# Float64 weights of a two-stage MoE: more raw chunks with places of their own, low parts subtracted by GpSimd, the factor 256 taken out of the split

## The chip, the cores and the metric

The kernel runs on one core of a Trainium2 chip. The metric is the device time of one execution in microseconds (us), smaller is better. The core has five engines with a queue each, run in order: TensorE (PE, with the weight load shown as PEld), VectorE (DVE), ScalarE (ACT), GpSimd (POOL) and SyncE (SP), which here issues the DMAs. Engines wait for each other through semaphores.

## The reference

```
def _moe_ref(x, w_a, w_b, w_out):
    a = x @ w_a
    b = x @ w_b
    return (a * b @ w_out).astype(np.float32)

def _moe2_ref(x, w_gate, w_val, w_out):
    gate = 1.0 / (1.0 + np.exp(-(x @ w_gate)))
    val = x @ w_val
    return (gate * val @ w_out).astype(np.float32)

def reference(**kwargs):
    attn_out = _attn_ref(**attn_kwargs)
    x = attn_out.transpose(0, 2, 1, 3).reshape(B * S, H * D)
    x = _moe_ref(x=x, **moe_kwargs)
    return _moe2_ref(x=x, **moe2_kwargs)
```

An attention of 4 batches, 8 heads, 576 positions of 64 (half of the heads see a local band of 32 positions, the other half every 32nd position) feeds two mixtures of 2304 tokens, 512 features and 1536 hidden features. The weights of both arrive as float64. The change is in the first mixture, a * b @ w_out.

## The kernel before, in words

**Tiles.** Tokens are worked in five tiles (four of 4 x 128 tokens, one of 4 x 64). For each tile the first mixture loops over 12 chunks k of 128 hidden features. Each chunk has three weights m of 128 x 512: m = 0 for a, m = 1 for b, m = 2 for the output. A product in fp32 accuracy is made of three passes in the type fp32r: high weight times high input, low weight times high input, high weight times low input, so each weight and each input is split in a high and a low part. On TensorE a chunk is 12 matmuls for a, 12 for b (line 1133) and 12 for the output (line 1224), the last for the chunk before.

**Conversion.** `convert` (line 495) turns each float64 weight into two fp32r parts, in the first tile only; the parts stay in 12 zones of SBUF, zone k for chunk k, and are used again by the later tiles. One weight goes through: `load` on SP (line 524, a DMA of 512 KB raw), `top` on ScalarE (530, the upper bits as a float), `merge` on VectorE (539, puts float32 bits together in place; what results is the weight times 1/256), `high_part` on ScalarE (547, times 256, rounded to fp32r) and `low_part` on VectorE (551, times 256, minus the high part). TensorE needs both parts.

**Places for raw weights.** Raw weights go to a ring of three slots (`raw`); a slot comes free when `low_part` has read it. The three weights of chunk 1 alone go to a place of their own, in zone 4, which is not needed for its own chunk yet. For these, `load` first has GpSimd copy one element from the raw weight of chunk 0 into the place (line 523), so that the load starts after that one has landed.

**Around it.** During the first tile VectorE and ScalarE also work the attention of the second tile: four groups of local heads (`attention`: TensorE's scores at line 628, VectorE's maximum at 640, ScalarE's exponentials at 646, VectorE's reciprocal and scaling at 652 to 661, TensorE's transposes at 669 and values at 685) and the strided heads (`strided`: products and sums on VectorE at 859 and 865, 922 and 929, then TensorE's transposes at 955). Between a and the output stands the gate (`gated`): ScalarE copies a out of PSUM (1280), VectorE multiplies by b (1154), ScalarE and VectorE split the result (1158, 1162).

**The order.** `Plan` places all operations before anything is emitted: each has an engine or a choice of them, a price in ns, dependencies, a key (when it should run) and ring slots. It always takes the operation that can start first, ties by key. So prices and dependencies set the order of each engine's queue; on the chip each queue runs in that order and waits where something is late. Chunks of TensorE's products are chained, small groups of the attention come between them where the plan found them ready.

Of the kernel before, what the change touches and what calls it, by code (L numbers as in the profile page):

```python
# [20 lines left out]
DM, DFF = 512, 1536  # L21
# [23 lines left out]
FRONT_KEYS = (-12, -11.9, -11.4, -11.3), (-9, -6), (-11.8, -11.7, -10)  # L45
R8 = 8
FIRST_KEY = -1
RAW_ZONE = 4
RB = R8 * TILES[0] // STRIDE

F_RING, V_RING, E_RING, T_RING = (0, 1), (2, 3, 4), (5, 6), (7,)
# [309 lines left out]
def r32(ap):  # L361
    return ap.bitcast(F32)
# [3 lines left out]
def attention_moe_kernel(ctx, tc, qkv, fqk, fvv, fq, fk, fv, sq, sk, sv, w1, w2, mask, ident, out):  # L366
# [128 lines left out]
    def convert(w, need, start=()):  # L495
        parts, done, merges = {}, {}, []
        tops, firsts = [], []

        def clear(op):
            for i in op.slot["c"]:  # L500
                tops.append(at(PLACE["c"] + i * DM, DM, FIRST, U32))
                POOL.memset(tops[-1], 0)

        c_top = add("POOL", 1000, clear, start, key=need(0, 0) - AHEAD - 10,
                    take=[("c", F_RING[:1]), ("c", F_RING[1:])])
        for c in range(3 * KF):
            k, m = divmod(c, 3)
            x = {}
            key = need(k, m) - AHEAD
            at_load = key - LEAD  # L510

            if k == 0 and m < 2:
                key -= EARLIER

            own = (RAW_ZONE * ZONE + m * 2 * DM, 2 * DM, EARLY) if k == 1 else None
            if k == 0:
                firsts.append(x)

            def load(op, x=x, k=k, m=m, own=own):

                x["raw"] = at(*own, U32) if own else raw(op, U32)[:, :2 * DM]
                if own:
                    POOL.tensor_copy(out=x["raw"][:1, :1], in_=firsts[m]["raw"][:1, 1:2])
                nc.sync.dma_start(
                    out=x["raw"].bitcast(U16)[:, :4 * DM - 1], in_=w[k, m].bitcast(U16)[:, 1:]
                )

            def top(op, x=x):
                x["t"] = tops[op.slot[f"t{id(w)}"][0]]
                ACT.activation(  # L530
                    out=x["t"].bitcast(F16).rearrange("p (n two) -> p n two", two=2)[:, :, 1],
                    in_=x["raw"].bitcast(BF16).rearrange("p (n four) -> p n four", four=4)[:, :, 2],
                    func=AF.Copy, scale=0.5,
                )

            def merge(op, x=x):
                u = x["raw"].rearrange("p (n two) -> p n two", two=2)[:, :, 0]
                x["f"] = u.bitcast(F32)
                DVE.scalar_tensor_tensor(  # L539
                    out=u, in0=u, scalar=13, in1=x["t"],  # L540
                    op0=ALU.logical_shift_right, op1=ALU.bitwise_or,
                )

            def high_part(op, x=x, k=k, m=m):
                hi, lo = (at(*weight(m, k, i), F32R) for i in range(2))
                parts[m, k] = hi, lo
                ACT.activation(out=hi, in_=x["f"], func=AF.Copy, scale=256.0)

            def low_part(op, x=x, k=k, m=m):
                hi, lo = parts[m, k]  # L550
                DVE.scalar_tensor_tensor(
                    out=lo, in0=x["f"], scalar=256.0, in1=r32(hi),
                    op0=ALU.mult, op1=ALU.subtract,
                )

            plan.slack = M2
            soon = w is w1 and k < 2
            taken = [] if own else [("raw", (0, 1, 2))]
            used = [own] if own else []
            after = [firsts[m]["op"]] if own else []  # L560
            a = touch(add("SP", 450, load, list(start) + after, key=at_load, take=taken, size=1 << 19), (), used)
            x["op"] = a
            b = touch(add("ACT", act(512) + 270 * soon, top, [a, c_top], key, take=[(f"t{id(w)}", (0, 1))]), used)
            end = c == 3 * KF - 1
            f = add("DVE", dve(512) + 90 * soon, merge, [b] + merges * end, key,
                    free=[(f"t{id(w)}", b)] + [("c", c_top)] * end)
            merges.append(f)
            touch(f, (), used)
            g = touch(add("ACT", act(512) + 160 * soon, high_part, [f], key), used, [weight(m, k, 0)])
            h = touch(add("DVE", dve(512) + 90 * soon, low_part, [g], key, free=[] if own else [("raw", a)]), used, [weight(m, k, 1)])  # L570
            done[m, k] = g, h
            plan.slack = 0
        return parts, done
# [615 lines left out]
    def evacuate(acc, key, nm, n, dst, after, ring):  # L1189

        ops = []
        for m in range(nm):
            y = {}

            def evac(op, m=m, y=y):
                y["y"] = small(op)[:, :n]
                if op.eng == "ACT":
                    ACT.copy(out=y["y"], in_=acc["bank"][m][:, :n])
                else:
                    DVE.tensor_copy(out=y["y"], in_=acc["bank"][m][:, :n])  # L1200

            def store(op, m=m, y=y):
                nc.sync.dma_start(out=dst(m), in_=y["y"])
# [34 lines left out]
    for i, n in enumerate(TILES):  # L1238
# [15 lines left out]
        for k in range(KF):  # L1254
# [22 lines left out]
                touch(pb[2], [(X0 + q * XZONE, XZONE, FIRST) for q in range(4)])  # L1277
            for m, v in enumerate((pa[2], pb[2])):
                touch(v, [weight(m, k, 0), weight(m, k, 1)])
            hh, hl = gated(x, key, n, pa, pb, lambda o, a: ACT.copy(out=o, in_=a))  # L1280
            if i == NJ - 1 and k == KF - 1:
                touch(hl, [(H0, 2 * N2, FIRST)])
            if pend:
# [539 lines left out]
```

## Time and profile before

| | |
|---|---|
| time before, median of 3 runs (lowest to highest) | 903.87 us (901.8 to 904.65) |
| profiled execution, its own time | 903.26 us |
| its span, from first to last instruction | 901.5 us |
| TensorE busy | 891.0 us, 99% |
| VectorE busy | 646.3 us, 72% |
| ScalarE busy | 409.9 us, 45% |
| GpSimd busy | 3.6 us, 15 instructions |
| TensorE's granted clock | 1.0 in all 40 slices |
| first mixture, first tile, about | 24 to 133 us |
| first mixture, other tiles, about | 133 to 435 us |

A row of the timeline has the start in us from the span's start, the length in us, engine, line, operation, output <- input, shape, and in brackets how long the engine was idle before and who ended that. Rows of two or more like instructions are merged (x2). Lines are those of the kernel before. The 1.8 us between span and time lie around the span and are taken as unchanged.

### The profile page before, as it was taken

How to read it: one execution, taken by the hardware profiler on the slowest of the kernel's cores; microseconds unless marked ns; L12 is line 12 of the kernel's file. 1: busy time of each engine (PE TensorE's matmuls, PEld its weight loads, DVE VectorE, ACT ScalarE, POOL GpSimd, SP SyncE). 2: the span in 40 equal slices, each digit the busy share in tenths (PEclk: the TensorE clock that was granted, in tenths of full speed). 3: DMA queues.
4: the chain of work that ended last, by engine and by line, in shares of the span. 5: the costliest groups of instructions: out<-in, count | busy, mean ns of one | idle time of the engine just before them, and what ended most of it. 6: DMA issues, size and time to landing. Idle time of an engine off the chain costs nothing.

```text
span 901.5 us, 14006 instructions
## 1 busy us (share of the span) xinstructions
PE 891.0 (99%) x5365; PEld 802.2 (89%) x5365; DVE 646.3 (72%) x1058; ACT 409.9 (45%) x857; POOL 3.6 (0%) x15
## 2 busy tenths in 40 slices
PE   8999999999999999999999999999999999999998
PEld 5787788888888888888899999999999999999998
DVE  5989998998999779811329876674768458659491
ACT  5766654411244113311236655564656545435351
POOL 0000000000000000000000000000000000000000
PEclk9999999999999999999999999999999999999999
DMA  9675665211242123300035243645675589943501
GB/s 311 209 234 188 200 199 165 91 44 59 80 134 78 57 65 125 115 1 1 1 118 164 94 141 123 204 155 187 212 230 181 182 301 334 378 167 115 167 18 62
DMA packets 60515, 132.72 MB, mean 147 GB/s; under 512 B 5728, under 2 KB 35040, under 8 KB 59552
## 3 DMA queue, kind: packets, MB, share of 16 engines
q1 hardware_dynamic: 60160, 131.60, 44.0%
q8 instruction: 42, 0.69, 0.3%
q10 hardware_dynamic: 288, 0.23, 0.1%
q14 instruction: 25, 0.20, 0.1%
HBM read 97.20 MB, written 34.60 MB: 146 GB/s over the span
## 4 chain that ended last, share of the span: by engine, by line
PE 89%; DVE 4%; DMA 4%; issue 1%; ACT 1%; SPq 1%; ACTq 0%; DVEq 0%
PE bank L1507 42%; PE bank L1133 29%; PE bank L1224 15%; DMA rest<-w 2%; PE bank L685 1%; PE bank L628 1%; DMA rest<-sq 1%; DMA w0p<-h2d 1%; PE bank L669 1%; DVE rest L539 1%; DMA w5p<-mask 1%; DVE s L865 0%; DVE rest L859 0%; PE bank L955 0%; DVE h16p L1162 0%
## 5 line engine op out<-in xcount | busy, mean ns | idle before, releaser
L1158 ACT CAST h16p<-rest 128x512 fp32r<-128x512 f32 (+1 forms) x60 | 34.6, 577 | 129.0 <-PE bank L1224 122.1
L1519 DVE TENSOR_TENSOR rest<-bank,rest 128x384 f32<-128x384 f32 x84 | 46.3, 555 | 57.6 <-PE bank L1507 33.0
L1154 DVE TENSOR_TENSOR rest<-bank,rest 128x512 f32<-128x512 f32 (+1 forms) x60 | 38.0, 634 | 55.4 <-PE bank L1133 55.0
L1280 ACT COPY rest<-bank 128x512 f32<-128x512 f32 (+1 forms) x60 | 32.6, 544 | 89.9 <-PE bank L1133 88.5
L1525 ACT COPY rest<-bank 128x384 f32<-128x384 f32 x84 | 40.1, 479 | 66.2 <-PE bank L1507 66.0
L1162 DVE TENSOR_TENSOR h16p<-rest,h16p 128x512 fp32r<-128x512 f32 (+1 forms) x60 | 38.2, 637 | 30.4 <-PE bank L1224 23.7
L859 DVE TENSOR_TENSOR rest<-rest 128x320 f32<-128x320 f32 (+13 forms) x56 | 51.6, 921 | 3.3 <-DMA rest<-sq 2.2
L922 DVE TENSOR_TENSOR rest<-rest,s 128x320 f32<-128x320 f32 (+13 forms) x56 | 51.5, 920 | 0.9
L929 DVE TENSOR_REDUCE rest<-rest 128x64 f32<-128x320 f32 (+13 forms) x56 | 51.3, 916 | 1.0
L865 DVE TENSOR_REDUCE s<-rest 128x5 f32<-128x320 f32 (+13 forms) x56 | 51.2, 914 | 1.0
L1417 DVE SCALAR_TENSOR_TENSOR rest<-rest 128x512 uint32<-128x512 uint32 x36 | 24.7, 689 | 10.6 <-ACT rest L1410 10.4
L1410 ACT ACTIVATE rest<-rest 128x512 f16<-128x512 bf16 x36 | 28.0, 790 | 5.8 <-DMA rest<-w 5.5
L530 ACT ACTIVATE rest<-rest 128x512 f16<-128x512 bf16 x33 | 25.8, 792 | 9.9 <-DMA rest<-w 9.5
L1529 ACT COPY bank<-bank 128x384 f32<-128x384 f32 x42 | 19.6, 466 | 20.5 <-PE bank L1507 20.2
L1590 DVE TENSOR_TENSOR rest<-bank,rest 128x384 f32<-128x384 f32 x36 | 20.1, 557 | 12.3 <-PE bank L1507 11.4
L1584 ACT ACTIVATE rest<-bank 128x384 f32<-128x384 f32 x36 | 17.7, 491 | 22.5 <-PE bank L1507 22.4
L646 ACT ACTIVATE rest<-bank,nm 128x96 f32<-128x96 f32 x56 | 18.3, 339 | 12.6 <-DVE nm L641 11.0
L539 DVE SCALAR_TENSOR_TENSOR rest<-rest 128x512 uint32<-128x512 uint32 x33 | 22.6, 687 | 1.3 <-ACT rest L530 1.2
L1584 ACT ACTIVATE rest<-rest 128x768 f32<-128x768 f32 x18 | 15.3, 847 | 14.1 <-DVE rest L1519 13.7
L1507 PE MATMUL bank<-w8p,w10p 128*128 128x384 f32 x100 | 20.7, 334 | 0.0
L1507 PEld LDWEIGHTS bank<-w8p,w10p 128*128 128x128 f32 x100 | 17.6, 188 | 0.0
L1507 PE MATMUL bank<-x15p,w3p 128*128 128x384 f32 x88 | 17.5, 334 | 0.0
(497 smaller groups left out, 2400.1 us busy)
## 6 DMA issues: line engine op xcount, KB each, us to landing
rest<-w SPq DMA_DIRECT2D x69, 511.8 KB, 4.3
h2d<-rest SPq DMA_DIRECT2D x18, 768.0 KB, 4.0
rest<-qkv SPq DMA_DIRECT2D x12, 416.0 KB, 4.2
w2p<-h2d SPq DMA_DIRECT2D x12, 384.0 KB, 5.1
w0p<-h2d SPq DMA_DIRECT2D x12, 384.0 KB, 5.5
w1p<-h2d SPq DMA_DIRECT2D x12, 384.0 KB, 5.1
out<-rest SPq DMA_DIRECT2D x24, 192.0 KB, 1.8
x2d<-rest SPq DMA_DIRECT2D x16, 256.0 KB, 2.2
```

Of the source, the lines that this page charges most:

```text
L859: engine[op.eng].tensor_tensor(out=product(op, n), in0=x["k", h][:, :, :n, :], in1=x["q"][h // 2][:, e:e + nh, j:j + 1, :].to_broadcast([P ...
L865: DVE.tensor_reduce(out=weights_of(h, j, n), in_=x["p", op.deps[0]], op=ALU.add, axis=AX.X)
L922: engine[op.eng].tensor_tensor(out=product(op, n, "p (h d t) -> p h d t"), in0=x["v", h][:, :, :, :n], in1=weights_of(h, j, n).unsqueeze(2 ...
L929: DVE.tensor_reduce(out=xs[:, j, e:e + nh, :], in_=x["p", op.deps[0]], op=ALU.add, axis=AX.X)
L1133: PE.matmul(x[tag][:, :n], ww[:, c * P:(c + 1) * P], xx(c), start=(u == 0 and c == chunks[0]), stop=(u == last and c == chunks[-1]),)
L1154: DVE.tensor_tensor(out=x["g"], in0=x["b"][:, :n], in1=x["g"], op=ALU.mult)
L1158: ACT.copy(out=x["hh"], in_=x["g"])
L1162: DVE.tensor_tensor(out=x["hl"], in0=x["g"], in1=r32(x["hh"]), op=ALU.subtract)
L1224: PE.matmul(ps[:, :n], ww[:, m * P:(m + 1) * P], x[xx], start=start, stop=stop)
L1507: PE.matmul(bank_of(where), at(*lhs(a, (0, 1, 0)[q], c), F32R), at(*rhs(b, (0, 0, 1)[q], c), F32R), start=p in OPENS and (q, c) == units[0 ...
L1519: DVE.tensor_tensor(out=at(*o), in0=bank_of("Z"), in1=at(*a), op=ALU.add)
L1525: "ACT", act2(NS), lambda op: ACT.copy(out=at(*o), in_=bank_of("Y")), [ops[after]], key - 20))
```

## The change

Three things change, all for the first mixture.

1. Chunks 1 to 4 have raw places of their own, in zones 4, 6, 7 and 5, instead of chunk 1 alone. Each of these loads is preceded by a GpSimd copy of one element out of the raw weight three loads earlier, and waits for that copy. The loads of chunks 5 to 11 and of chunk 0 use the ring of three.
2. `low_part` of chunks 1 to 11 is a GpSimd subtraction; that of chunk 0 stays on VectorE. The plan's price for it is 1500 ns.
3. `high_part` is a copy without the factor 256, so both parts are of the weight divided by 256. The factor comes back where sums leave PSUM: 256 for a in the gate (which makes up for a's weights; b's and the output's remain), and 65536 in `evacuate`.

```
-RAW_ZONE = 4
+RAW_ZONES = {1: 4, 2: 6, 3: 7, 4: 5}
...
-            own = (RAW_ZONE * ZONE + m * 2 * DM, 2 * DM, EARLY) if k == 1 else None
-            if k == 0:
-                firsts.append(x)
-
-            def load(op, x=x, k=k, m=m, own=own):
+            own = (RAW_ZONES[k] * ZONE + m * 2 * DM, 2 * DM, EARLY) if k in RAW_ZONES else None
+            before = firsts[-3] if own else None
+            firsts.append(x)
+
+            def load(op, x=x, k=k, m=m, own=own, before=before):
...
-                    POOL.tensor_copy(out=x["raw"][:1, :1], in_=firsts[m]["raw"][:1, 1:2])
+                    POOL.tensor_copy(out=x["raw"][:1, :1], in_=before["raw"][:1, 1:2])
...
-                ACT.activation(out=hi, in_=x["f"], func=AF.Copy, scale=256.0)
+                ACT.copy(out=hi, in_=x["f"])
...
-                DVE.scalar_tensor_tensor(
-                    out=lo, in0=x["f"], scalar=256.0, in1=r32(hi),
-                    op0=ALU.mult, op1=ALU.subtract,
-                )
+                engine[op.eng].tensor_tensor(out=lo, in0=x["f"], in1=r32(hi), op=ALU.subtract)
...
-            after = [firsts[m]["op"]] if own else []
+            after = [before["op"]] if own else []
...
-            h = touch(add("DVE", dve(512) + 90 * soon, low_part, [g], key, free=[] if own else [("raw", a)]), used, [weight(m, k, 1)])
+            h = touch(add(*(("DVE", dve(512) + 90) if k == 0 else ("POOL", 1500)), low_part, [g], key, free=[] if own else [("raw", a)]), used, [weight(m, k, 1)])
...
-                    ACT.copy(out=y["y"], in_=acc["bank"][m][:, :n])
+                    ACT.activation(out=y["y"], in_=acc["bank"][m][:, :n], func=AF.Copy, scale=float(2 ** 16))
...
-                    DVE.tensor_copy(out=y["y"], in_=acc["bank"][m][:, :n])
+                    DVE.tensor_scalar_mul(y["y"], acc["bank"][m][:, :n], float(2 ** 16))
...
-            hh, hl = gated(x, key, n, pa, pb, lambda o, a: ACT.copy(out=o, in_=a))
+            hh, hl = gated(x, key, n, pa, pb, lambda o, a: ACT.activation(out=o, in_=a, func=AF.Copy, scale=256.0))
```

Lines up to 551 keep their numbers; from 555 on, a line of the changed kernel is three lower (669 is 666 there, 859 is 856). As the plan sees other prices and dependencies, the order of the queues changes. GpSimd's whole queue between the first memset of `convert` and the end of the conversion was:

```order
L502 MEMSET rest 128x512 x2
L523 COPY w4p_80<-rest 1x1 x3
L810 MEMSET s_405 128x128
L810 MEMSET s_1361 128x192
L810 MEMSET s_1996 128x256
```

and is now, to the subtractions of chunk 3 (w4p, w6p, w7p and w5p are the raw places, w1p to w3p the parts, s the strided scores):

```order
L502 MEMSET rest 128x512 x2
L523 COPY w4p_80<-rest 1x1 x3
L523 COPY w6p_82<-w4p_80 1x1
L807 MEMSET s_407 128x128
L523 COPY w6p_82<-w4p_80 1x1 x2
L523 COPY w7p_83<-w6p_82 1x1
L551 ISA
L551 TENSOR_TENSOR w1p_477<-w4p_80,w1p_477 128x512 x3
L523 COPY w7p_83<-w6p_82 1x1 x2
L523 COPY w5p_81<-w7p_83 1x1
L551 TENSOR_TENSOR w2p_573<-w6p_82,w2p_573 128x512 x3
L523 COPY w5p_81<-w7p_83 1x1
```

Copies and subtractions stand in one queue now, with an ISA row ahead of the first subtraction, which the built program names a reload of the library of code for GpSimd. The subtractions of chunks 4 to 11 follow three by three.

SP's queue behind the three loads of chunk 1 (w4p) was this (sq, sk and qkv are loads of the attention):

```order
L524 DMA w4p_80<-w 128x2047 x3
L524 DMA rest<-w 128x2047
L845 DMA rest<-sq 128x2x256
L600 DMA rest<-qkv 128x832
L608 DMA rest<-qkv 96x512
L821 DMA rest<-sk 128x512
L524 DMA rest<-w 128x2047
```

and is now:

```order
L524 DMA w4p_80<-w 128x2047 x3
L524 DMA w6p_82<-w 128x2047
L524 DMA rest<-w 128x2047
L842 DMA rest<-sq 128x2x256
L597 DMA rest<-qkv 128x832
L605 DMA rest<-qkv 96x512
L818 DMA rest<-sk 128x512
L524 DMA w6p_82<-w 128x2047 x2
L524 DMA w7p_83<-w 128x2047
```

The loads named w6p are chunk 2, w7p chunk 3; those into rest are chunk 2 before and chunk 5 now.

VectorE's queue from the gate multiplication of chunk 2 to the scaling (line 661, now 658) that TensorE's transposes in chunk 3 wait for was:

```order
L1154 TENSOR_TENSOR rest<-bank_630,rest 128x512
L859 TENSOR_TENSOR rest<-rest 128x384
L652 TENSOR_SCALAR nm_639<-nm_639 128x4
L653 RECIPROCAL nm_639<-nm_639 128x4
L551 SCALAR_TENSOR_TENSOR w3p_664<-rest,w3p_664 128x512
L661 TENSOR_TENSOR rest<-rest,nm_639 128x384
```

and is now:

```order
L1151 TENSOR_TENSOR rest<-bank_627,rest 128x512
L694 TENSOR_TENSOR x14p_288<-bank_637,x12p_285 128x2x128
L539 SCALAR_TENSOR_TENSOR w7p_83<-w7p_83,rest 128x512
L856 TENSOR_TENSOR rest<-rest 128x512
L1159 TENSOR_TENSOR h16p_513<-rest,h16p_513 128x512
L649 TENSOR_SCALAR nm_677<-nm_677 128x4
L650 RECIPROCAL nm_677<-nm_677 128x4
L862 TENSOR_REDUCE s_407<-rest 128x8
L658 TENSOR_TENSOR rest<-rest,nm_677 128x384
```

The subtraction is gone, and merges and strided products that stood behind the scaling stand ahead of it. On TensorE the transposes that wait for it stand behind 12 of the 24 products of chunk 3 (4 before), 12 of chunk 4 (4 before) and 16 of chunk 5 (12 before); those of the strided heads stand in the middle of chunk 8 (20 products into chunk 9 before) and ahead of chunk 11 (behind the last product of the tile's output before).

## Rows read from the trace of the kernel before

**Rows 1.** The page, part 1: busy time, share of the span, instructions of TensorE.
```profile
PE 891.0 (99%) x5365; PEld 802.2 (89%) x5365; DVE 646.3 (72%) x1058; ACT 409.9 (45%) x857; POOL 3.6 (0%) x15
```

**Rows 2.** Windows: stretch, length, busy time by engine, clock, DMA share, GB/s.
```profile
28.00:133.00 105.00, 103.46 (x565) 82.39 (x563) 96.83 (x185) 68.43 (x135) 0.26 (x1) 1.00 0.64 205
133.00:435.00 302.00, 302.00 (x1615) 246.33 (x1614) 231.88 (x319) 84.62 (x226) 0.53 (x2) 1.00 0.25 77
```

**Rows 3.** Timeline of TensorE: start, length, engine, line, operation [idle before, releaser].
```profile
50.52 0.62 PE L1133 MATMUL bank<-x12p,w3p 128*128 128x512 f32 x2
...
60.45 0.62 PE L1133 MATMUL bank<-x12p,w4p 128*128 128x512 f32 x2
...
70.39 0.61 PE L1133 MATMUL bank<-x12p,w5p 128*128 128x512 f32 x2
...
74.17 0.61 PE L669 MATMUL bank<-idt,rest 128*96 128x128 f32 x4 [0.53 <-DVE rest L661]
...
82.29 0.61 PE L1133 MATMUL bank<-x12p,w6p 128*128 128x512 f32 x2
...
90.45 0.61 PE L1133 MATMUL bank<-x12p,w7p 128*128 128x512 f32 x2
...
107.00 0.62 PE L1133 MATMUL bank<-x12p,w9p 128*128 128x512 f32 x2
...
116.09 0.61 PE L1133 MATMUL bank<-x12p,w10p 128*128 128x512 f32 x2
```

**Rows 4.** Line 551: duration min/median/max in ns, first and last start.
```profile
L551 DVE SCALAR_TENSOR_TENSOR w1p<-w4p,w1p x3: 681/683/685, 28.4 to 35.2; 128x512 fp32r<-128x512 f32 x3
```

**Rows 5.** Timeline of VectorE: two gate multiplications, pitch of 512 and 320 columns.
```profile
38.14 0.69 DVE L1154 TENSOR_TENSOR rest<-bank,rest 128x512 f32<-128x512 f32 x1
...
42.07 0.69 DVE L859 TENSOR_TENSOR rest<-rest 128x512 f32<-128x512 f32 x1
42.67 0.69 DVE L539 SCALAR_TENSOR_TENSOR rest<-rest 128x512 uint32<-128x512 uint32 x1
...
45.07 0.49 DVE L859 TENSOR_TENSOR rest<-rest 128x320 f32<-128x320 f32 x1
45.47 0.55 DVE L640 TENSOR_REDUCE nm<-bank 128x4 f32<-128x384 f32 x1
...
48.00 0.69 DVE L1154 TENSOR_TENSOR rest<-bank,rest 128x512 f32<-128x512 f32 x1 [0.46 <-PE bank L1133]
```

**Rows 6.** DMA issues of 5 to 60 us: KB each, median us to landing.
```profile
rest<-w SPq DMA_DIRECT2D x13, 511.8 KB, 6.1
...
w4p<-w SPq DMA_DIRECT2D x3, 511.8 KB, 4.9
...
w8p<-fvv SPq DMA_DIRECT2D x1, 384.0 KB, 9.2
```

**Rows 7.** Timeline of all engines, first 45 us.
```profile
0.73 0.99 POOL L502 MEMSET rest<- 128x512 uint32 x2 [0.29 <-POOLq L1810]
...
1.66 1.28 ACT L469 ACT_TABLE_LOAD   x1 [1.66 <-PEq L1810]
...
16.52 3.87 SPq L524 DMA_DIRECT2D w4p<-w  x3
...
27.61 0.66 ACT L547 ACTIVATE w1p<-w4p 128x512 fp32r<-128x512 f32 x1
...
32.49 0.62 PE L1133 MATMUL bank<-x12p,w1p 128*128 128x512 f32 x2
```

**Rows 8.** Timeline, 16 to 20 us: a GpSimd copy alone, one beside VectorE.
```profile
16.32 0.17 POOL L523 COPY w4p<-rest 1x1 uint32<-1x1 uint32 x1 [14.61 <-DMA rest<-w]
...
19.84 0.36 DVE L652 TENSOR_SCALAR nm<-nm 128x4 f32<-128x4 f32 x1
19.85 0.19 POOL L523 COPY w4p<-rest 1x1 uint32<-1x1 uint32 x1 [1.07 <-DMA rest<-w]
```

**Rows 9.** Line 652 over the whole span: duration min/median/max in ns.
```profile
L652 DVE TENSOR_SCALAR nm<-nm x20: 138/162/364, 10.8 to 380.7; 128x4 f32<-128x4 f32 x16, 128x2 f32<-128x2 f32 x4
```

## The prediction

> **What bounds the kernel now.** I read the page first: TensorE is busy for 99% of the span [rows 1], so a change can save only where TensorE waits, and can cost wherever it makes TensorE wait. The windows say where: from 133 to 435 us it never rests; from 28 to 133 us, the first token tile of the first MoE, 1.5 us are missing, with VectorE busy for 96.8 of 105 us [rows 2]. Busy time hides part of a wait, since ends of matmuls are modelled, so I went to the timeline and took starts of weight chunks [rows 3]. Chunk 6 runs from 82.29 to 90.45: 36 products with nothing between, 8.16 us, 0.227 us each. Chunk 4 takes 9.94 us, with three small groups of the attention between its products, so 0.6 us for each group. Chunk 5, with two groups, should take 9.36 and takes 11.90: 2.5 us are lost, part of them seen at 74.17, where line 669 waited for VectorE's line 661. Chunk 9, with one group, takes 9.09 instead of 8.76: 0.3 more. **2.8 us are all that a better flow of weights can give here.**
>
> **What the change takes away.** 33 subtractions leave VectorE, 0.68 us long [rows 4]; VectorE starts instructions of 512 columns every 0.60 us (42.07 to 42.67) and of 320 every 0.40 [rows 5], so 33 × 0.60 = 20 us of its 97 go. Chunks 2, 3 and 4 no longer wait for a slot of the ring of three: 9 loads move ahead, each still started by a GpSimd copy that waits for the landing of the load three before. Chunk 5 then finds the ring free. Its parts, which come last now, should come some microseconds earlier, and the 2.8 us go if nothing else is late. Further on, a slot of the ring is held for landing, ScalarE, VectorE, ScalarE and now GpSimd, so each turn is longer by the difference of 1.2 and 0.68; six turns use up 3 us of that lead and not all of it. I put no cost there.
>
> **The first subtraction on GpSimd.** GpSimd's order has a library load (the ISA row) ahead of it, and ahead of that a copy which waits for the first load of chunk 2. That load starts when the first of chunk 1 has landed: 16.52 + 4.9 = 21.4 [rows 6, 7]. It lands about 4.9 later, at 26.4, and the ISA starts at 26.6. ScalarE's high part is there at 27.61 + 0.66 = 28.3, and TensorE wants the low part at 32.49 [rows 7]; VectorE's subtraction of it started at 28.4 [rows 4]. No row shows such a load. The nearest rows are ScalarE's table load, 1.28 us [rows 7], and landings of DMAs in this busy stretch, 6.1 us at the median and 9.2 at most [rows 6]. The subtraction itself is bounded by GpSimd's memset of as many columns, 0.5 us each, which only writes [rows 7], and by three such passes, two reads and a write, 1.5; I take 1.2, near the upper end, since it is the same engine with all three streams. With 1.28 nothing waits. With 9.2 the part comes at 37.0 and TensorE waits 4.5. I take 6.1, the ordinary fetch of that stretch: 26.6 + 6.1 + 1.2 = 33.9, a wait of **1.4 us**. The Trainium skill (GPSIMD Engine Reference, Instruction dispatch) says that the first call to a freshly loaded kernel pays some 6 us which no instruction in the profile shows; by it the wait would be 1.3, an estimate that no run here shows yet.
>
> **What GpSimd does to VectorE.** The trace has one place where a GpSimd instruction that reads ran beside a VectorE instruction of its neighbourhood: at 19.84 line 652 took 0.36 us while a copy of 0.19 ran on GpSimd from 19.85 [rows 8]; the median of its 20 is 0.16 [rows 9]. So VectorE stood for about as long as the copy took. The subtractions are six times that long and there are 33. Lower bound of the hold: nothing. Upper bound: 1.2 us each, 40 us in all, twice what VectorE is relieved of. By the counts of its new order about 60% of VectorE's time goes to instructions with two SBUF inputs (lines 539, 856, 1159, 658, 919), and it would be busy for (97 - 20)/105 = 73%; 0.73 × 0.6 × 1.2 = 0.53, less what reductions and PSUM reads can run underneath: I take **0.4 us** for each.
>
> Does that reach TensorE? VectorE's new order has pulled the strided products forward, so it isn't slack. Between the gate multiplication of chunk 1 (ends 38.74) and that of chunk 2, which TensorE releases at 48.00 [rows 5], there are 9.3 us, and 19 instructions that take 9.0 by the pitch of 0.40 to 0.60. Four subtractions fall in there: 4 × 0.4 = 1.6, so VectorE is 1.3 late. From that multiplication to line 658, for which TensorE's transposes of line 666 wait, stand 8 more instructions, 3.5 us: 48.6 + 3.5 + 0.4 + 1.3 = 53.8. TensorE is there after 12 products of chunk 3, at 50.52 + 2.72 = 53.24 [rows 3]: it waits 0.6. In the next stretch, to the release at 60.45 - 2.72 = 57.8, 7.8 us of work and 1.6 of holds meet 9.2 us: 1.5 late, and at chunk 4 (58.4 + 3.3 + 0.4 + 1.5 = 63.6 against 60.45 + 2.72 + 0.6) no wait. In the third, to 67.7, 8.5 and 1.6 meet 9.3: 2.3 late; the transposes stand behind 16 products now, at 70.39 + 3.6 + 0.6 = 74.6, and line 658 is done 4.1 + 0.4 + 2.3 after 68.3, at 75.1: 0.5. All these times move together with the 1.4 us above. **Waits of 1.1 us.**
>
> **Edits at nothing.** ScalarE's high part is a copy without a factor, and the factors 256 and 65536 come along in copies out of PSUM that exist already; none of these is waited for by TensorE in the steady rows (82.29 to 90.45), and the cover, 3 us or more until the next use of a bank, would have to go before it cost 0.05 us apiece. The three subtractions of chunk 0 stay on VectorE. The second MoE's order is the same on all engines.
>
> **Sum:** -2.8 + 1.4 + 1.1 = -0.3. The profiled execution took 903.26, so **903.0 us**; the median of the three runs shown is 903.87, and a few tenths of that are chance. A measurement of this kernel tells a change from none at about 0.3%, 2.7 us.
>
> **Rivals.** *It flows.* The library comes in within 4.7 us (26.6 to 32.49, less 1.2) and holds stay at 0.2 or less, since reductions and reads of PSUM run underneath. For it: ScalarE's table load took 1.28, and the copy at 16.32 [rows 8] held nothing visible. Against it: the row at 19.84, and DMA queues that are full at 25 to 30 us. Then all of the 2.8 comes: 900.5.
>
> *GpSimd holds VectorE* for most of each subtraction, so that work is not moved but doubled. With 0.8 us each the same three stretches are late by 2.9, 4.7 and 7.1 us; TensorE waits 2.6, 1.4 and 2.3 at line 666 of chunks 3, 4 and 5, with the 1.4 of the start 7.7 us, less 2.8: 908.2. It decides from about 0.65 us of hold; with the full 1.2 it would be 913. For it: row 19.84, where the hold was whole. Against: there VectorE's instruction was of another kind. Weighed against a rule: the Trainium skill (SBUF — State Buffer, Who interferes with whom) has VectorE and GpSimd share a port pair as an exclusive lock, and a VectorE instruction with two SBUF inputs contend with a GpSimd instruction that reads. By that rule this rival is what happens; the row agrees in the length of the hold, and no row shows the rule for two inputs.
>
> *The library is late.* At the longest landing, 9.2 us, TensorE waits 4.5: -2.8 + 4.5 + 1.1, 906.1. For it: everything behind the ISA on GpSimd waits as well, the copies for chunks 3 and 4 and so SP's queue behind these loads. Against: 9.2 was met by one DMA of many.
>
> **Chances.** Forecast, with what lies around it within 2.7 us: 0.42. It flows: 0.27, since two bounds must both fall low. Hold: 0.22. Late library: 0.09. So faster 0.27, same 0.42, slower 0.31. The range starts below the first rival, at 899.9, for the tenths by which runs differ, and goes to 908.5, past the hold of 0.8; what is left out above is a hold near the full length or a library beyond 10 us, about 0.15. The forecast's own range is 901 to 905.5.
>
> **What would show it.** In the timeline of the changed kernel: the ISA near 26.6 and the first subtraction of chunk 1 ending near 33.9, with TensorE's third pair of chunk 1 waiting for GpSimd; subtractions near 1.2 us; in the windows VectorE's busy time from 28 to 133 about 97 - 20 + 13; lines 856 and 1159 longer than 0.49 to 0.69 where a subtraction runs; chunk 5 near 9.4 to 10 us. I am wrong if lines 666 or 952 make TensorE wait for more than 3 us, if the first low part is there before 32.5, or if TensorE waits in the stages behind 133 us.

## The result and the profile of the changed kernel

**912.23 us** (median of 5 runs, 911.81 to 915.29) against 904.01 for the kernel before in the same comparison (5 runs, 901.8 to 905.96): a ratio of 1.0101, with a 95% interval of 1.0085 to 1.0116. The change makes the kernel slower by 1%. The forecast was 903.0 with a range up to 908.5.

The page's parts 1 and 2 for the changed kernel, beside [rows 1]: busy time by engine, and GpSimd's in 40 slices.

```profile
PE 895.7 (98%) x5365; PEld 805.4 (88%) x5365; DVE 649.9 (71%) x1025; ACT 407.5 (45%) x854; POOL 53.1 (6%) x57
...
POOL 0354341000000000000000000000000000000000
```

GpSimd works 53 us instead of 3.6, all in the first sixth of the span, and VectorE, which lost 33 subtractions, is busy for 649.9 us instead of 646.3. So the work that left VectorE came back as longer instructions. Where TensorE pays for it is read from its timeline (columns as in [rows 3]; here the first product of chunk 1, the waits of over 0.5 us, and the first product of the next tile):

```profile
35.48 0.73 PE L1130 MATMUL bank<-x12p,w1p 128*128 128x512 f32 x2
...
61.37 0.73 PE L666 MATMUL bank<-idt,rest 128*96 128x128 f32 x4 [3.66 <-DVE rest L658]
...
74.52 0.61 PE L666 MATMUL bank<-idt,rest 128*96 128x128 f32 x4 [1.47 <-DVE rest L658]
...
87.06 0.61 PE L666 MATMUL bank<-idt,rest 128*96 128x128 f32 x4 [1.52 <-DVE rest L658]
...
130.63 0.73 PE L1130 MATMUL bank<-x12p,w10p 128*128 128x512 f32 x2 [0.99 <-DVE rest L1151]
...
145.78 0.62 PE L1130 MATMUL bank<-x12p,w0p 128*128 128x512 f32 x2
```

In the kernel before, the first and the last of these were:

```profile
31.45 0.73 PE L1133 MATMUL bank<-x12p,w1p 128*128 128x512 f32 x2
...
132.93 0.71 PE L1133 MATMUL bank<-x12p,w0p 128*128 128x512 f32 x2
```

From chunk 1 to the next tile it is 110.30 us against 101.48, 8.8 more. Three of the waits are for line 658, the scaling that VectorE has to finish before TensorE's transposes of line 666. The first wait, 3.66 us, costs more than itself. The windows (columns as in [rows 2]: stretch, length, TensorE, weight load, VectorE, ScalarE, GpSimd, clock, DMA share, GB/s) show TensorE's granted clock at 0.50 behind it, the 1.2 GHz level:

```profile
20.00:24.00 4.00, 4.00 (x72) 2.52 (x71) 2.85 (x9) 1.67 (x4) 0.49 (x3) 0.60 0.84 248
24.00:28.00 4.00, 4.00 (x42) 2.96 (x40) 1.90 (x5) 2.21 (x6) 0.52 (x3) 0.55 0.62 234
...
62.00:64.00 2.00, 2.00 (x6) 1.55 (x6) 1.66 (x4) 2.00 (x4) 0.00 (x0) 0.50 0.00 0
```

and TensorE's products there come at a pitch of 1.00 and 0.85 us for a pair. In chunk 6 of the kernel before, a pair takes 0.45 (8.16 us for 18 pairs [rows 3]):

```profile
61.75 1.20 PE L1130 MATMUL bank<-x12p,w3p 128*128 128x512 f32 x2
62.75 1.05 PE L1130 MATMUL bank<-x13p,w3p 128*128 128x512 f32 x2
63.60 1.05 PE L1130 MATMUL bank<-x12p,w3p 128*128 128x512 f32 x2
64.45 0.95 PE L1130 MATMUL bank<-x13p,w3p 128*128 128x512 f32 x2
```

The pitches are 0.55 + 0.40 + 0.40 over, and two small groups behind them lose 0.3: some 1.7 us by the clock. The same view shows a low clock from 20 to 28 us as well, and this execution, at 915.29 the slowest of the five, reaches chunk 1 only at 35.48. The kernel of the first experiment, with the same queues up to there, all but GpSimd's memsets, reaches it at 31.96; two other kernels below in which GpSimd subtracts (one raw place, hold in the plan) reach it at 29.95 and 32.02. So this late start is not put down to the change, and I compare the stretch from chunk 1 on, and the medians.

VectorE's timeline from the gate multiplication of chunk 1 to the scaling that TensorE waits for at 61.37:

```profile
43.21 0.68 DVE L1151 TENSOR_TENSOR rest<-bank,rest 128x512 f32<-128x512 f32 x1
...
49.56 1.78 DVE L539 SCALAR_TENSOR_TENSOR w7p<-w7p,rest 128x512 uint32<-128x512 uint32 x1
51.27 0.47 DVE L862 TENSOR_REDUCE s<-rest 128x5 f32<-128x320 f32 x1
...
55.70 0.68 DVE L1151 TENSOR_TENSOR rest<-bank,rest 128x512 f32<-128x512 f32 x1
...
58.72 1.25 DVE L649 TENSOR_SCALAR nm<-nm 128x4 f32<-128x4 f32 x1
...
60.10 0.65 DVE L862 TENSOR_REDUCE s<-rest 128x8 f32<-128x512 f32 x1
60.67 0.55 DVE L658 TENSOR_TENSOR rest<-rest,nm 128x384 f32<-128x384 f32 x1
```

and GpSimd's (the last copy ahead of the first subtraction, that subtraction, and those that fall in this stretch):

```profile
27.76 0.17 POOL L523 COPY w7p<-w6p 1x1 uint32<-1x1 uint32 x1 [1.14 <-DMA w6p<-w]
32.39 1.32 POOL L551 TENSOR_TENSOR w1p<-w4p,w1p 128x512 fp32r<-128x512 f32 x1 [4.45 <-ACT w1p L547]
...
47.72 3.08 POOL L551 TENSOR_TENSOR w2p<-w6p,w2p 128x512 fp32r<-128x512 f32 x2 [3.23 <-ACT w2p L547]
...
58.36 1.59 POOL L551 TENSOR_TENSOR w3p<-w7p,w3p 128x512 fp32r<-128x512 f32 x1 [1.32 <-ACT w3p L547]
```

Line 539, a merge with two tensors from SBUF, takes 1.78 us at 49.56, over the end of two subtractions, instead of 0.69 [rows 5]; line 649, which adds a constant to 128x4 values, takes 1.25 us at 58.72 instead of 0.16 [rows 9], until the subtraction that began at 58.36 is through. The reductions (51.27, 60.10) and the gate multiplication, which reads PSUM (55.70), keep their length. The groups of lines from 28 to 140 us say the same for the whole stage (busy time, mean ns of one | idle before):

```profile
L1159 DVE TENSOR_TENSOR h16p<-rest,h16p 128x512 fp32r<-128x512 f32 x10 | 11.9, 1194 | 0.0
...
L862 DVE TENSOR_REDUCE s<-rest 128x5 f32<-128x320 f32 (+3 forms) x16 | 9.2, 578 | 0.2
L1151 DVE TENSOR_TENSOR rest<-bank,rest 128x512 f32<-128x512 f32 x11 | 7.5, 684 | 0.7 <-PE bank L1130 0.7
...
L649 DVE TENSOR_SCALAR nm<-nm 128x4 f32<-128x4 f32 x4 | 2.3, 569 | 0.0
```

Line 1159 took 690 ns in the kernel before. If every VectorE instruction between 24 and 150 us is compared with the mean of the same line and shape in the kernel before, the excess is **21.5 us, 0.65 for each of the 33 subtractions**. What VectorE was relieved of is 33 x 0.60 = 20 us. The excess sits where a subtraction runs: 37 of VectorE's 89 instructions with two inputs in SBUF overlap a subtraction in time, and these are 19.8 us longer in sum; 25 reductions, reads of PSUM and reciprocals overlap one too, and are not longer (0.0 us in sum).

### The profile page after: what moved, and what is told of

Same layout as the page of the kernel before. It is cut to its first block, busy times and chain, and to the rows that moved or that the text cites. A ratio compares the mean times of both kernels' runs of the same rounds, so it can differ in the third digit from the quotient of the medians.

```text
span 913.5 us, 14056 instructions
## 1 busy us (share of the span) xinstructions
PE 895.7 (98%) x5365; PEld 805.4 (88%) x5365; DVE 649.9 (71%) x1025; ACT 407.5 (45%) x854; POOL 53.1 (6%) x57
## 4 chain that ended last, share of the span: by engine, by line
PE 84%; DVE 0%; ACT 0%; issue 0%
PE bank L1504 43%; PE bank L1130 26%; PE bank L1221 13%; PE bank L682 1%; PE bank L625 1%; PE bank L666 0%; PE bank L952 0%; DVE w4p L1460 0%; DVE rest L1516 0%; ACT w4p L1457 0%; DVE rest L1587 0%; ACT rest L1277 0%; PE bank L478 0%; DVE h16p L1345 0%; DVE w3p L1460 0%
## 5 line engine op out<-in xcount | busy, mean ns | idle before, releaser
L1277 ACT ACTIVATE rest<-bank 128x512 f32<-128x512 f32 (+1 forms) x60 | 33.2, 554 | 95.1 <-PE bank L1130 93.7
L1159 DVE TENSOR_TENSOR h16p<-rest,h16p 128x512 fp32r<-128x512 f32 (+1 forms) x60 | 43.5, 724 | 28.3 <-PE bank L1221 21.5
L919 DVE TENSOR_TENSOR rest<-rest,s 128x320 f32<-128x320 f32 (+13 forms) x56 | 56.7, 1013 | 1.1
L856 DVE TENSOR_TENSOR rest<-rest 128x320 f32<-128x320 f32 (+13 forms) x56 | 54.5, 972 | 2.4 <-DMA rest<-sk 0.7
L1414 DVE SCALAR_TENSOR_TENSOR rest<-rest 128x512 uint32<-128x512 uint32 x36 | 24.7, 688 | 11.4 <-ACT rest L1407 11.3
L1407 ACT ACTIVATE rest<-rest 128x512 f16<-128x512 bf16 x36 | 28.0, 789 | 6.2 <-DMA rest<-w 6.1
L539 DVE SCALAR_TENSOR_TENSOR rest<-rest 128x512 uint32<-128x512 uint32 x24 | 17.4, 724 | 4.8 <-issue 3.6
L530 ACT ACTIVATE rest<-rest 128x512 f16<-128x512 bf16 x24 | 18.6, 789 | 0.3 <-DMA rest<-w 0.2
L1587 DVE TENSOR_TENSOR rest<-rest 128x768 f32<-128x768 f32 x18 | 17.1, 953 | 0.8 <-DVE rest L1516 0.5
```

The costliest lines, as they stand in the source:

```text
L856: engine[op.eng].tensor_tensor(out=product(op, n), in0=x["k", h][:, :, :n, :], in1=x["q"][h // 2][:, e:e + nh, j:j + 1, :].to_broadcast([P ...
L919: engine[op.eng].tensor_tensor(out=product(op, n, "p (h d t) -> p h d t"), in0=x["v", h][:, :, :, :n], in1=weights_of(h, j, n).unsqueeze(2 ...
L1159: DVE.tensor_tensor(out=x["hl"], in0=x["g"], in1=r32(x["hh"]), op=ALU.subtract)
L1587: DVE.tensor_tensor(out=at(*o), in0=src(), in1=at(*o), op=ALU.mult)
```

## The experiments

All edits are to the changed kernel. "Stage" is the time from the first product of chunk 1 to that of the next tile in the profile; "holds" is the excess of VectorE's instructions, worked out as above; the ratio is to the kernel before, with its 95% interval.

| kernel | stage, us | holds, us | median, us | ratio |
|---|---|---|---|---|
| before | 101.48 | 0 | 901.6 to 904.0 | 1 |
| changed | 110.30 | 21.5 | 912.23 | 1.0101 (1.0085 to 1.0116) |
| GpSimd only writes | 98.61 | 1.8 | 900.51 | 0.9982 (0.9968 to 0.9997) |
| GpSimd copies once | 100.26 | 3.7 | 901.42 | 0.9997 (0.9987 to 1.0007) |
| GpSimd copies twice | 101.85 | 11.5 | 903.57 | 1.0009 (0.9994 to 1.0024) |
| low parts on VectorE | 99.42 | none | 901.54 | 0.9991 (0.9978 to 1.0004) |
| one raw place | 109.81 | 17.4 | 911.01 | 1.0098 (1.0067 to 1.0129) |
| one subtraction in three | 103.49 | 6.6 | 904.97 | 1.0028 (1.0017 to 1.0040) |
| hold in the plan | 113.89 | 19.9 | 915.57 | 1.0153 (1.0134 to 1.0172) |
| strided work later | 99.93 | none | 900.66 | 0.9993 (0.9981 to 1.0005) |

### GpSimd as busy, but without reading

```
-                engine[op.eng].tensor_tensor(out=lo, in0=x["f"], in1=r32(hi), op=ALU.subtract)
+                DVE.tensor_tensor(...) if k == 0 else [POOL.memset(lo.bitcast(U32), 0) for _ in range(3)]
```

> The changed kernel with every queue in the same order, but each of the 33 GpSimd subtractions is replaced by three memsets of the same 512 columns (about 3 x 0.5 us), so GpSimd is as busy and only writes; the low parts of chunks 1 to 11 are left out of the result. Theory A (GpSimd's reads hold VectorE's instructions that take two tensors from SBUF, and the small TENSOR_SCALAR): line 1159 falls from 1.19 us to 0.69, line 649 from 0.57 to 0.16, TensorE's waits of 3.66, 1.47 and 1.52 us for line 658 shrink to under 0.6 each, and with them the spell at the lower clock goes; time 901 to 903. Rival B (the new order is too tight in itself: transposes behind 12 products where VectorE can't have their input): waits and time stay, 910 to 913. Rival C (GpSimd's own queue is late, whatever it does): stays near 912 too, with waits released by GpSimd.

Measured: 900.51 us, ratio 0.9982, a little below the range expected. All queues but GpSimd's are the same, GpSimd is busy for some 50 us with memsets (they wait for less than the subtractions and run earlier in the stage), and the timeline marks no wait of TensorE from 22 to 146 us. VectorE's groups, 28 to 140 us:

```profile
L1159 DVE TENSOR_TENSOR h16p<-rest,h16p 128x512 fp32r<-128x512 f32 x12 | 8.2, 687 | 3.9 <-PE bank L1221 3.9
...
L649 DVE TENSOR_SCALAR nm<-nm 128x4 f32<-128x4 f32 x5 | 1.8, 360 | 0.0
```

Line 1159 is back at 0.69, though 50 of VectorE's 97 two-input instructions overlap a memset in time; they are 0.02 us longer in sum. So theory A holds, and B falls, as the order is the same. C falls less directly, since the memsets wait for less: in the changed kernel no marked wait of TensorE from chunk 1 on is ended by GpSimd, and the two copies below, which wait for the high part as the subtractions do, make 903.57 us. Line 649 is not quite back: 0.36 against 0.16. The stage, from these two rows of TensorE, is 98.61 us:

```profile
31.96 0.73 PE L1130 MATMUL bank<-x12p,w1p 128*128 128x512 f32 x2
...
130.57 0.62 PE L1130 MATMUL bank<-x12p,w0p 128*128 128x512 f32 x2
```

That is 2.87 less than before: the flow of weights does give back what the prediction counted, 2.8. The measured ratio, 0.3 to 2.9 us under the kernel before, agrees. But the order has next to no room, as VectorE's gate multiplication of chunk 2 and its scaling for chunk 3 show:

```profile
48.85 0.69 DVE L1151 TENSOR_TENSOR rest<-bank,rest 128x512 f32<-128x512 f32 x1
...
52.94 0.55 DVE L658 TENSOR_TENSOR rest<-rest,nm 128x384 f32<-128x384 f32 x1
```

The scaling ends at 53.49, and TensorE's transposes are due at 53.74, 12 products (2.72 us) into chunk 3, which starts at 51.02. So in this order TensorE waits as soon as line 658 ends more than a quarter of a microsecond later than in this run.

### One copy, and two

```
-                engine[op.eng].tensor_tensor(out=lo, in0=x["f"], in1=r32(hi), op=ALU.subtract)
+                DVE.tensor_tensor(...) if k == 0 else POOL.tensor_copy(out=lo, in_=x["f"])
```

> The changed kernel in the same order, but GpSimd copies the merged weight into the low part: one tensor read instead of two, no library load ahead of it; the low parts of chunks 1 to 11 are left out of the result. If any read of GpSimd holds VectorE for the instruction's own length: the copy's duration d against 1.32 us gives holds of about 21 us x d / 1.32 in sum, and a time between 901 and 912 in the same proportion (0.9 us: 908). If only a second read holds: VectorE's line 1159 at 0.69 as with memsets, 900 to 902.

Measured: 901.42, ratio 0.9997. A copy takes 0.63 us alone and up to 1.05 beside VectorE:

```profile
27.95 0.63 POOL L551 CAST w1p<-w4p 128x512 fp32r<-128x512 f32 x1
...
41.03 1.05 POOL L551 CAST w2p<-w6p 128x512 fp32r<-128x512 f32 x1 [3.08 <-DVE w6p L539]
```

Holds are 3.7 us, a third of the 10 that the proportion gave, and the time is below the range expected for it. The time lies in the range of the second answer, but line 1159 took 0.79 on the mean and not 0.69, so neither answer stood as written. This copy also starts earlier, as it doesn't wait for the high part. The next run takes that away (`[POOL.tensor_copy(out=lo, in_=r32(hi)) for _ in range(2)]` in the same place):

> The changed kernel in the same order, but in place of each subtraction GpSimd copies the high part into the low part twice: it waits for the high part as the subtraction does and is busy about as long (2 x 0.63 us against 1.32), with one tensor read at a time; the low parts of chunks 1 to 11 are left out of the result. With a single copy the holds were 3.7 us in sum. If it is the second read of the subtraction that shuts VectorE out: holds near 2 x 3.7 = 7 us or less, 900 to 904. If it is how long GpSimd reads and where in VectorE's order that falls: holds near 20 us and 909 to 913.

Measured: 903.57, ratio 1.0009. The time lies in the range of the first answer, the holds between the two: 11.5 us, 0.35 for each pair, about half of what a subtraction of nearly the same length holds. About as much of VectorE's two-input work lies beside GpSimd as in the changed kernel (28.0 us of overlap with the copies, 29.1 with the subtractions). GpSimd, then TensorE:

```profile
28.01 1.29 POOL L551 CAST w1p<-w1p 128x512 fp32r<-128x512 f32 x2 [1.29 <-ACT w1p L547]
```

```profile
54.00 0.61 PE L666 MATMUL bank<-idt,rest 128*96 128x128 f32 x4 [0.93 <-DVE rest L658]
...
77.16 0.61 PE L666 MATMUL bank<-idt,rest 128*96 128x128 f32 x4 [1.06 <-DVE rest L658]
```

So a hold grows with the time GpSimd reads and with where that falls, and a subtraction holds more than two copies of one input. Whether that is its second read or the seam between the copies was not tried apart. The two runs and the first give a scale in the one order: 1.8, 3.7, 11.5 and 21.5 us of holds make stages of 98.61, 100.26, 101.85 and 110.30.

### Low parts on VectorE again

```
-            h = touch(add(*(("DVE", dve(512) + 90) if k == 0 else ("POOL", 1500)), low_part, ...
+            h = touch(add("DVE", dve(512) + 90 * soon, low_part, ...
```

> The changed kernel with the low parts of all chunks on VectorE again; raw places of chunks 1 to 4 and the factor taken out of the split stay. The plan then puts the transposes of the local heads behind 16, 24 and 24 products of chunks 3 to 5. Theory A: no holds, line 1159 at 0.69, the loss of 2.5 us in chunk 5 of the kernel before is gone because its parts no longer wait for the ring: 900.5 to 902.5. If the raw places or the factor were what costs (rival D): 908 or more. If VectorE, busy for 97 of 105 us again, makes TensorE wait somewhere else: 903 to 905.

Measured: 901.54, ratio 0.9991: not to be told from the kernel before, and 1% under the change. Raw places and factor cost nothing that these runs can show (interval 0.9978 to 1.0004), so rival D falls. The stage is 2.1 us shorter than before. What is missing to 2.87 is in chunk 2:

```profile
44.68 0.73 PE L1130 MATMUL bank<-x12p,w2p 128*128 128x512 f32 x2 [0.75 <-ACT w2p L547]
```

The raw weight had landed by 36.6 us, when a GpSimd copy that waits for it ran; its merge ran at 42.08, behind strided products in VectorE's queue, which had no gap from 35 us on.

### One raw place, with GpSimd's subtractions

```
-RAW_ZONES = {1: 4, 2: 6, 3: 7, 4: 5}
+RAW_ZONES = {1: 4}
```

> The changed kernel with a raw place for chunk 1 alone, as before; low parts of chunks 1 to 11 on GpSimd, factor out of the split. Transposes stand behind 4, 4 and 8 products of chunks 3 to 5. Theory A: holds of about 0.65 us per subtraction as in the changed kernel, and the ring of three is held longer, so TensorE waits for parts as well as for line 658: 909 to 918. Rival D (raw places are what costs): 903 to 905.

Measured: 911.01, as theory A has it, with holds of 0.53 us for each subtraction. The slowness comes with the subtractions, whatever the places; the two longest waits of TensorE are again for line 658:

```profile
53.26 1.06 PE L666 MATMUL bank<-idt,rest 128*96 128x128 f32 x4 [2.06 <-DVE rest L658]
...
78.76 0.61 PE L666 MATMUL bank<-idt,rest 128*96 128x128 f32 x4 [2.94 <-DVE rest L658]
```

### One subtraction in three

```
-            h = touch(add(*(("DVE", dve(512) + 90) if k == 0 else ("POOL", 1500)), low_part, ...
+            h = touch(add(*(("POOL", 1500) if k and m == 2 else ("DVE", dve(512) + 90 * soon)), low_part, ...
```

> The changed kernel with GpSimd subtracting only the low part of the output weight of chunks 1 to 11: 11 subtractions instead of 33; the rest on VectorE. Transposes behind 12, 24 and 24 products of chunks 3 to 5. Theory A with a cost that is a threshold (VectorE's lateness counts only once its slack in front of line 658 is used up): VectorE is held for about 7 us in all, TensorE waits under 1 us, 901 to 903. Theory A with a cost in proportion (a third of the 11 us between 901 and 912): 904 to 906.

Measured: 904.97, the case of a cost in proportion. Eleven subtractions hold VectorE for 6.6 us, 0.60 each, and the stage is 4.1 us longer than with all low parts on VectorE. TensorE's longest waits moved to the strided heads:

```profile
106.02 0.33 PE L952 MATMUL bank<-idt,rest 128*128 128x128 f32 x1 [1.55 <-DVE rest L926]
...
126.58 0.33 PE L952 MATMUL bank<-idt,rest 128*128 128x128 f32 x1 [0.82 <-DVE rest L926]
```

Even a third of the dose was not free.

### The plan told of the hold

```
-            f = add("DVE", dve(512) + 90 * soon, merge, ...
+            f = add("DVE", dve(512) + 90 * soon + 650 * (k > 0), merge, ...
```

> The changed kernel, but the plan is told of the hold: each merge of chunks 1 to 11 is priced 650 ns dearer on VectorE (21.5 us of longer VectorE instructions in the changed kernel's trace, over 33 subtractions). The operations are the same; TensorE's transposes move behind 12, 24, 24 and 24 products of chunks 2 to 5. If the loss comes from an order that was made without the hold (theory A, VectorE late in front of line 658): holds stay at about 20 us in sum, waits for line 658 go to under 0.5 us, no spell at the lower clock, 901 to 904. If the holds cost in themselves, wherever the transposes stand, since VectorE has no less to do than before: waits move to other lines (gate, merge, strided transposes) and the time stays at 906 to 912.

Measured: 915.57, slower still and past both ranges; the second reading is the nearer one. The waits for line 658 are gone but for one of 0.64. In their place TensorE waits for parts, above all in chunks 10 and 11 (TensorE's timeline; SP's waits of 60 to 147 us: total, times, longest; the window of 94 to 147 us):

```profile
124.57 0.73 PE L1130 MATMUL bank<-x12p,w10p 128*128 128x512 f32 x2 [1.73 <-ACT w10p L547]
...
136.41 0.73 PE L1130 MATMUL bank<-x12p,w11p 128*128 128x512 f32 x2 [0.99 <-ACT w11p L547]
```

```profile
SPq L524 <- POOL w10p L551: 8.6, 3, 6.2
```

```profile
94.00:147.00 53.00, 47.31 (x193) 36.05 (x194) 40.65 (x55) 25.28 (x41) 23.17 (x16) 0.97 0.56 178
```

VectorE is busy for 40.7 of 53 us there, so it isn't the bound. SP's loads wait for GpSimd's low parts to free the ring of three, up to 6.2 us at a time for chunk 10's (and 9.7 for chunk 5's). The holds are as large as before (19.9). A dearer price in the plan moved the waits and did not remove them; which of its effects on the order does most was not taken apart.

### Versions for speed

Three versions with low parts on VectorE were to get the last 0.8 us of the flow. The first starts the strided heads two weights later in the chain of conversions, after m = 0 of chunk 1 instead of m = 1 of chunk 0 (`[done1[0, 1][0]]` in place of `[done1[1, 0][0]]` for `start`):

> Low parts on VectorE as in the run before, raw places and factor as in the change, and the strided heads' work starts with the high part of chunk 1's second weight's predecessor in the chain of parts one chunk of work later (after the high part of m = 0, k = 1), so that merges of chunk 2 stand ahead of strided products in VectorE's queue. Theory: the 1.05 us that TensorE lost in chunk 2 with low parts on VectorE (line 547 waited for merges behind strided products) goes, and nothing else comes late: about 1 us under that run, 900 to 901.5, faster than before by 0.1 to 0.3%. Rival: strided work now ends too late for its transposes in chunks 9 and 11: 902 to 904.

Measured: 900.66, ratio 0.9993. Chunk 2 takes 9.92 us, so its wait is gone, and chunk 4 has one instead:

```profile
61.47 0.72 PE L1130 MATMUL bank<-x12p,w4p 128*128 128x512 f32 x2 [1.24 <-DVE w4p L551]
```

The others price chunk 2 as dear as chunks 0 and 1 (`soon = w is w1 and k < 3`), without and with that later start:

> Low parts on VectorE, raw places and factor as in the change, and chunk 2 priced as dear as chunks 0 and 1 in the plan (90 ns more on VectorE, 270 and 160 on ScalarE). The transposes move to 12, 20 and 20 products of chunks 3 to 5. Theory: the 1.05 us lost in chunk 2 with low parts on VectorE shrinks: 900 to 901.5. Rival: it only moves to the next chunk, as with strided work put off (1.24 us there in chunk 4): 901 to 903.

> As the run before, and strided work put off by one weight as well. The transposes stand behind 16, 16, 20 and 24 products of chunks 2 to 5. Theory: no wait over 0.5 us from 30 to 133 us, the whole 2.8 us of the flow: first mixture's first tile as short as with memsets on GpSimd (98.6 us from chunk 1 to the next tile), 899.5 to 901. Rival: chunk 4's low parts are late again, 900.5 to 902.

Measured: 902.77, ratio 1.0000 (0.9985 to 1.0016), stage 99.87; and 904.02, ratio 1.0008 (0.9991 to 1.0024), stage 100.29, with a wait of 1.37 us in chunk 3. The last time lies above both ranges expected for it. Each time the wait moves to another place. All versions with low parts on VectorE beat the change, and none can be told from the kernel before.

## Why the prediction was wrong

- **"2.8 us are all that a better flow of weights can give here"** was right: with GpSimd writing only, the stage is 2.87 us shorter.
- **The library load, 1.4 us**, did not happen as a cost. The last copy ended at 27.93, the first subtraction began at 32.39. ScalarE's high part, which it needs, ended 0.08 us earlier:

```profile
31.63 0.68 ACT L547 CAST w1p<-w4p 128x512 fp32r<-128x512 f32 x1
```

  So the load took at most 4.5 us where I took 6.1, and TensorE, which wanted that part at 36.52 in this execution, never waited. In the kernel with the hold in the plan, where the high part came earlier, GpSimd was idle for 0.53 us between the copy and the first subtraction, so there the load held nothing for longer than that:

```profile
29.57 1.35 POOL L551 TENSOR_TENSOR w1p<-w4p,w1p 128x512 fp32r<-128x512 f32 x1 [0.53 <-ACT w1p L547]
```

  The rule of the Trainium skill (GPSIMD Engine Reference, Instruction dispatch) on some 6 us for the first call is not borne out by these traces.
- **The subtraction, 1.2 us**: measured 1.32 alone, 1.42 in the mean of the 33.
- **One step that failed is the hold, "0.4 us for each"**. It measured 0.65, which is the very value that the prediction named as the point from which the rival "GpSimd holds VectorE" decides. The working was 0.73 x 0.6 x 1.2, less something for reductions and PSUM reads. The 0.73 was VectorE's busy share without holds, but a queue that is held falls behind and does not rest: VectorE was busy for 97.0 of 105 us, 0.92. With that and 1.32 us the product is 0.73, near the 0.65. And the 0.6 had left reductions and PSUM reads out already, so taking them off again counted them twice.

```profile
28.00:133.00 105.00, 97.08 (x588) 76.79 (x585) 97.00 (x150) 64.91 (x134) 44.61 (x35) 0.98 0.56 190
...
147.00:435.00 288.00, 288.00 (x1554) 235.03 (x1553) 226.18 (x311) 81.09 (x218) 0.53 (x2) 1.00 0.25 77
```

- **The step that cost more is the one from holds to TensorE, "Waits of 1.1 us".** With 0.65 put into the same three stretches, TensorE would wait 3.8 us in all, and the sum would be 905.7, still inside the range. Measured against the memset run, which has the same order, TensorE lost 11.7 us. Two copies show the same: they hold 0.35 each and make the stage 3.2 us longer than memsets do. For chunk 3 the working had three things wrong. It let VectorE begin the first stretch on time, at the gate multiplication of chunk 1. But in the changed kernel two instructions ahead of that multiplication were held for over 1 us each (the rows below, beside 0.49 and 0.69), and the multiplication started 7.73 us after the first product of chunk 1, against 6.68 in the memset run, 1.05 later:

```profile
36.20 1.51 DVE L856 TENSOR_TENSOR rest<-rest 128x320 f32<-128x320 f32 x1
37.64 1.80 DVE L1159 TENSOR_TENSOR h16p<-rest,h16p 128x512 fp32r<-128x512 f32 x1
```

  It counted four subtractions up to the gate multiplication of chunk 2, which is what came, and one from there to line 658, where there are two (55.73 and 58.36). And it gave VectorE 1.1 us of room in front of line 658. The run with memsets shows 0.25: the gate multiplication of chunk 2 starts there at 48.85, at once behind another instruction, where I had put it at 48.00 (48.5 in that run, in which chunk 3 starts 0.5 us later). Together line 658 ends 4.21 us later after chunk 1's first product than with memsets (25.74 against 21.53); less the 0.28 that TensorE had lost in chunk 2 and the 0.25 of room, that leaves 3.7, and TensorE waited 3.66.
- Two slips in the sums of the working, small beside that: the forecast adds the wait in chunk 5 to that in chunk 3 though TensorE is 0.6 us later by then (0.6 instead of 1.1), and the rival at 0.8 us leaves out, in chunks 4 and 5, the 0.6 us of a small group that the forecast counts (907.6 instead of 908.2).
- **The clock was in no term.** In the profiled execution a wait of 3.66 us was followed by a granted clock of 0.50, and 1.7 us went there.
- Put together by chunks, against the memset run with the same order: 0.3 in chunk 2, 5.4 in chunk 3 (3.66 and the clock), 1.65 in chunk 4, 1.7 in chunk 5, 2.2 in chunk 10, 0.5 in others, 11.7 in all. The sum looked at chunks 3 to 5 alone; the 2.2 of chunk 10, where the longest wait (0.99 us) is for a gate multiplication, were at nothing in it. With the flow's -2.87 that is the 8.8 us by which the stage is longer, and the medians differ by 8.2. The prediction's own sign of being wrong came true: line 666 made TensorE wait 6.65 us, more than 3.
- The rival's mechanism was the right one, and so was the rule it was weighed against (the Trainium skill, SBUF — State Buffer, Who interferes with whom): two-input VectorE instructions are held by a GpSimd that reads, and stay at 0.69 beside one that only writes. Its price was too low as well: it had 908.2 at 0.8 us, and 0.65 made 912.23. I gave it 0.22 because the only row that showed a hold [rows 8] was of another kind of instruction. That row was evidence for it, in full length, and deserved more.
- Right besides: from 147 to 435 us TensorE has no gap, the factor cost nothing that the run with low parts on VectorE could show, and chunk 6 takes 8.16 us as before.

## What to carry to other kernels

In this kernel, a subtraction moved from VectorE to GpSimd was only moved where VectorE, meanwhile, ran reductions, PSUM reads or nothing. Here 20 us of subtractions left VectorE and 21.5 us of holds came back. As a first estimate, price such a move at the whole length of the GpSimd subtraction times the share of time in which VectorE runs instructions that can be held (0.73 by that, 0.65 measured; small one-input ones are among them, and copies held about half as much). Then add holds along the whole stage, not in a few places, and look at the room in front of each instruction that TensorE waits for before calling any of it hidden. A probe that keeps GpSimd as busy with memsets in the same order tells the hold from the order in one run.

## What the runs showed of the hardware that was not expected

- A VectorE addition of a constant to 128x4 values, with one SBUF input (line 649), is held by GpSimd's reads (0.57 us mean, 1.25 at most, against 0.16) and even by its memsets (0.36), beside which instructions with two inputs keep their 0.69. The Trainium skill (SBUF — State Buffer, Who interferes with whom) names such operations among those that can take both ports and so contend; the numbers agree.
- It goes both ways: GpSimd's copy of 512 columns took 0.63 us alone and up to 1.05 beside VectorE, and a pair of subtractions 3.08 instead of 2.64.
- One stall of 3.66 us of TensorE cost 1.7 us more through the granted clock; the stalls of 1.47 and 1.52 us in the same trace were followed by products at the full pitch. The length of the stall alone does not tell which it will be: with one raw place a wait of 2.06 us was followed by a granted clock of 0.50 (54 to 56 us) and one of 2.94 us by 1.00 (79 to 82 us), and with the hold in the plan one of 1.73 us, with one of 0.49 behind it, by 0.50 (127 to 129 us).
